# Query norms in a work bank, x transposes one round later, two weight transfers in smaller pieces

## The chip, the core and the metric

The kernel runs on one core of a Trainium2 chip. A core has five engines with instruction queues of their own: PE (TensorE, matrix multiplication), DVE (VectorE), ACT (ScalarE), POOL (GpSimd) and SP (SyncE, which here only issues transfers). They meet at semaphores. PE writes to PSUM[...]; everything else lies in SBUF or in device memory. The metric is the device time of one execution in microseconds.

## The reference, cut to what matters

Attention with normalised queries and keys feeds a layer of experts, in which each token takes one of eight experts besides a dense branch:

```python
q_n, k_n = rmsnorm(q, g_q), rmsnorm(k, g_k)      # (8, 12, 448, 64)
attn = softmax(scale * q_n @ k_n.T)
x = (attn @ v).transpose(0, 2, 1, 3).reshape(B * S, H * D)   # 3584 x 768
y_dense = relu(x @ w1_dense) @ w2_dense           # F = 512
expert_idx = argmax(x @ w_gate, axis=1)           # 8 experts
y_moe[mask] = gate_w[mask] * (relu(x[mask] @ w1[e]) @ w2[e])
return y_dense + y_moe
```

## The kernel before, in words

The kernel has two stages. The first computes attention and, between its own steps, the first half of the dense branch, the router's logits, each token's expert and its place among the expert's tokens. It writes one record per token to device memory. The second stage gathers the records by expert, 128 tokens at a time, and computes the rest. The change touches the first stage, and what both stages call to load weights.

Attention works in groups of four heads, 24 groups in all; three groups make a batch. `period(g)` is one turn of the loop. It has J = 7 rounds (i from 0 to 6), and in each of them PE computes a set of scores for group g + 1 (`scores`, L282) and ACT takes their exp (L285). Besides, the period multiplies the exps of group g with the values in two halves (`attend`, L303, rounds 1 and 2, then 4 and 5), divides each half by its sums (`divide`, L310 and L313, rounds 3 and 6), transposes the queries and keys of group g + 2 (L260, round 3) and copies them out of PSUM (L268, L270, round 4), squares and sums those of g + 3 (L226, L233), turns the sums into norms (`norms`, ACT, L241 to L245) and multiplies queries (DVE) and keys (POOL) with them (`normalise`, L251, round 6). The output x of group g - 2 is transposed (`xtrans`, L323) and copied out (`xturned`, L329).

Work of other kinds comes once per batch. The logits and the choice of expert (L348, L357 to L366) come in round 5 of the third period of a batch, the ranks and places (L383, L392 to L406) in round 5 of the first. The dense branch is done in fills of six matrix multiplications (`fill`, `dense`, L474), each followed by a relu on ACT (`relu`, L485): one at the end of round 6 in every period, and a second one at the end of round 5 in the second period of a batch. Fills begin with the fifth period, logits with the sixth, ranks with the seventh. The norms stop three groups before the end.

The order on every engine is the order in which the code is written: the stage is scheduled by hand, and each engine executes its queue in that order. Waits come from the tiles: an instruction waits for those that use the same tile, or the same buffer of a rotating pool.

[...]The scores have two tiles of two banks. The products with the values have one tile `av` of two banks, each with 260 of its 512 columns in use. The pool `wk` ("work banks") has two banks, handed out in turn to whatever asks next: the x transposes (`xt`), the transposes of queries and of keys (`tr`), the bank `R` of logits or ranks, and each fill (`ff`). Who gets a bank waits until its last reader is done. The norms of the queries, 14 columns, have no bank of their own: they lie behind the products in the first bank of `av` (`rq`, L161). The norms of the keys lie in SBUF.

The weights of the experts come through POOL's queue (`wjobs`), 16 matrices of 1.5 MB read and 768 KB written as bf16. Eleven of them are issued in the periods (L522). The last five lie over memory that the exps use, so they are issued after attention by `late_weight`, which cuts every second matrix, those of the shape 512 x 768, into pieces of one row of 3 KB.

Of the kernel before, what the change touches and what calls it, by code (L numbers as in the profile page):

```python
# [9 lines left out]
F32 = mybir.dt.float32  # L10
# [9 lines left out]
def kernel(  # L20
# [14 lines left out]
    nc = tc.nc  # L35
    P = 128
    B, H, S, D = q.shape
    N = B * S
    Dm = H * D
    E = moe_w_gate.shape[1]  # L40
    F = moe_w1_dense.shape[1]
    J = 7
    NPR = H // 2
    NT = B * NPR
    GP = 2
# [88 lines left out]
        wjobs.append((we[:, e, 1].rearrange("p (fo d) -> p fo d", d=Dm),  # L134
                      moe_w2[e].rearrange("(p fo) d -> p fo d", p=P)))

    def late_weight(i):

        o, w = wjobs[i]
        if i % 2:  # L140
            nc.gpsimd.dma_start(o, w, max_dma_last_dim=4 * Dm)
        else:
            nc.gpsimd.dma_start(o, w)
# [6 lines left out]
    with tc.tile_pool(name="a_ld", bufs=2) as ld, \  # L150
# [4 lines left out]
        tail = [False]  # L155
        xin, sqs, ssqs, rs, xn, qkT, exs, xas, xTs, avs, trs, xps = [{} for _ in range(12)]


        av = avp.tile([P, GP, 512], F32, name="av")
        SP0 = 4 * De  # L160
        rq = av[:, 0, SP0:SP0 + 2 * J].rearrange("p (h j) -> p h j", h=2)  # L161
        def scratch():


# [72 lines left out]
        def norms(g):  # L237
            if g >= NG:
                return
            ln = sb.tile([P, 2, 2, J], F32, tag="ln", name="ln")  # L240
            nc.scalar.activation(ln, ssqs[g], AF.Ln, bias=eps_t, scale=1.0 / D)  # L241
            rs["q"] = rq
            rs["k"] = sb.tile([P, 2, J], F32, tag="r", name="r")
            nc.scalar.activation(rq, ln[:, 0], AF.Exp, scale=-0.5)  # L244
            nc.scalar.activation(rs["k"], ln[:, 1], AF.Exp, scale=-0.5)  # L245
# [60 lines left out]
        def divide(g, hh):  # L306
            b, gb = divmod(g, NPR // GP)
            avv = avs[hh]
            inv = sb.tile([P, GP, 4, 1], F32, tag="inv")
            nc.vector.reciprocal(inv, avv[:, :, :, D:])  # L310
            o = xas[b].rearrange("p m (a c i d) -> p m a i c d", a=NA, c=2, d=D // 2)
            for c in range(2):
                nc.vector.tensor_mul(  # L313
                    o[:, :, gb, 2 * hh:2 * hh + 2, c].rearrange("p m r d -> p r m d"),
                    avv[:, :, :, c * D // 2:(c + 1) * D // 2],
                    inv.to_broadcast([P, GP, 4, D // 2]))
# [177 lines left out]
        def period(g):  # L494
            b, gb = divmod(g, NB)
            for i in range(J):
                if i == 6:
                    divide(g, 1)
                if i > 0:
                    relu()  # L500
                if g + 1 < NG:
                    scores(g + 1, i)
                if i == 0:
                    if g > 1:
                        xtrans(g - 2)
                    squares(g + 3, "k")
                    sums(g + 3, "q")
                if i == 5:
                    if gb == 0 and b > 1:
                        ranks(b - 2)  # L510
                        places(b - 2)
                    if gb == 2 and b > 0:
                        logits(b - 1)
                        choose(b - 1)
                if i in (1, 2, 4, 5):
                    for m in range(2):
                        attend(g, i // 3, (i - 1) % 3 * 2 + m)
                if i == 1:
                    if g > 1:
                        xturned(g - 2)  # L520
                    while nw[0] < len(wjobs) - LATE and (nw[0] - 2) * WPACE <= g + 1:
                        nc.gpsimd.dma_start(*wjobs[nw[0]])  # L522
                        nw[0] += 1
                if i == 3:
                    if g + 2 < NG:
                        transposes(g + 2, "q")
                        transposes(g + 2, "k")
                    divide(g, 0)
                    sums(g + 3, "k")
                    values(g + 2)  # L530
                    squares(g + 4, "q")
                    load(g + 5)
                if i == 4:
                    if g + 2 < NG:
                        turned(g + 2, "q")
                        turned(g + 2, "k")
                if i == 5 and gb == 1:
                    fill(g, KD)
                if i == 6:
                    norms(g + 3)  # L540
                    normalise(g + 3, "q")
                    normalise(g + 3, "k")
                    if gb == 2:
                        store(b, 0, XH, xas[b].bitcast(F32))
                    if gb == 0 and b > 1:
                        gates(b - 2)
                    load_v(g + 4)
                    fill(g, KD)
# [11 lines left out]
        def run(order):  # L560
            with tc.manual_schedule(engines=order):
                for g in range(2):
                    load(g)
                load_v(0)
                load(2)
                load_v(1)
                constants()
                setup()

                squares(0, "q", scalar=True)  # L570
                sums(0, "q")
                squares(0, "k", scalar=True)
                sums(0, "k")
                norms(0)
                normalise(0, "q")
                normalise(0, "k")
                transposes(0, "q")
                transposes(0, "k")
                nc.vector.tensor_mul(gqk, gq2, gk2)
                turned(0, "q")  # L580
                turned(0, "k")
                squares(1, "q", scalar=True)
                sums(1, "q")
                squares(1, "k", scalar=True)
                sums(1, "k")
                values(0)
                squares(2, "q")
                for j in range(J):
                    scores(0, j)
                    if j == 0:  # L590
                        norms(1)
                        normalise(1, "q")
                        normalise(1, "k")
                        load(3)
                        sums(2, "q")
                        squares(2, "k")
                    if j == 2:
                        transposes(1, "q")
                        transposes(1, "k")
                        turned(1, "q")  # L600
                        turned(1, "k")
                        values(1)
                        sums(2, "k")
                        squares(3, "q")
                        load(4)
                    if j == 5:
                        norms(2)
                        normalise(2, "q")
                        normalise(2, "k")
                load_v(2)  # L610
                load_v(3)
                for job in wjobs[:3]:
                    nc.gpsimd.dma_start(*job)
                for g in range(NG - 1):
                    period(g)

                g = NG - 1
                tail[0] = True  # L620
                gts = []
                for i in (-5, -4):
                    late_weight(i)
                for _ in range(2):
                    gts.append(ld.tile([P, 4, RC - GO], F32, tag="xv", name="gt"))
                    nc.gpsimd.memset(gts[-1], 0.0)
                xtrans(g - 2)
                logits(B - 2)
                for hh in range(2):
                    for m in range(4):  # L630
                        attend(g, hh, m)
                    if hh == 0:
                        xturned(g - 2)
                        choose(B - 2)
                        xtrans(g - 1)
                relu()
                divide(g, 0)
                xturned(g - 1)
                ranks(B - 2)
                divide(g, 1)  # L640
                store(B - 1, 0, XH, xas[B - 1].bitcast(F32))
                xtrans(g)
                places(B - 2, (0, 1))
                xturned(g)
                places(B - 2, (2,))
                logits(B - 1)
                fill(g, KD)
                choose(B - 1)
                relu()
                places(B - 2, (3,))  # L650
                ranks(B - 1)
                gates(B - 2, gts[0])
                gates(B - 1, gts[1])
                fill(NG + 1, 8 * KD)
                relu()
                tables()
# [3 lines left out]
    with tc.tile_pool(name="m_sb", bufs=5) as sb, \  # L660
# [76 lines left out]
        def slots(t0, t1):  # L737
# [3 lines left out]
            if t0 == 0:  # L741


                for i in (-3, -2, -1):
                    late_weight(i)
            for t in range(t0 + here, min(t0 + ahead, t1)):
                turn(t)
            turn_here(t0, 0)
# [57 lines left out]
```

## Time and profile before

| | before |
|---|---|
| time, median of 3 runs | 405.2 us (404.52 to 413.1) |
| profiled run, span | 403.5 us |
| PE busy | 344.0 us (85%) |
| DVE, ACT, POOL busy | 226.4, 216.4, 217.3 us |
| granted PE clock | 0.968 |
| attention stage, until its last scores | 224 us |
| PE busy from 50 to 200 us, of 10 us each | 8.24 to 9.86 |

The profile shows one execution. "Busy" is the share of time in which an engine had an instruction in work; for each group of instructions it also tells how long the engine stood idle just before, and which instruction of which engine ended that idle time. In the lines, `xn<-xq,av` means that `xn` was written from `xq` and `av`; L numbers are lines of the kernel before. A row of the timeline gives the start, the duration, the engine, the line and, in brackets, the idle time ahead of it and what ended it. Nearly all of the second stage has PE busy throughout; the attention stage does not.

### The profile page before, as it was taken

What the parts mean: (1) busy time and instruction counts of PE and PEld (TensorE: products, weight loads), DVE (VectorE), ACT (ScalarE), POOL (GpSimd) and SP (SyncE); (2) the same over time, 40 slices, a digit from 0 to 9 for tenths busy, and PEclk for the clock granted to TensorE, in tenths of its full rate; (3) what the DMA queues carried; (4) which work ended last, traced back from release to release, by engine and by line L of the source; (5) the groups of instructions that cost most, each with busy time, mean ns of one, the idle gap of its engine ahead of it and who ended that gap; (6) DMA issues with size and microseconds to landing.
All of it is one profiled execution on the core that took longest, in us unless ns stands there. A gap on an engine that the chain in (4) does not pass through costs nothing. (4 is left out here: it accounts for less than half of the span.)

```text
span 403.5 us, 13022 instructions
## 1 busy us (share of the span) xinstructions
PE 344.0 (85%) x5250; PEld 209.7 (52%) x5250; DVE 226.4 (56%) x554; ACT 216.4 (54%) x349; POOL 217.3 (54%) x193
## 2 busy tenths in 40 slices
PE   0688789989899898899899893799999999999990
PEld 0355565655556555555466542465555555555550
DVE  3856897887978978978786672232212121212220
ACT  4576988778788787787788321122322222222220
POOL 4896797765777676666661102534454545444220
PEclk9996999999999999999999987799999999999997
DMA  7899798959899698899672853999999999999921
GB/s 238 288 249 274 209 257 269 256 144 334 193 280 259 187 255 259 224 278 237 187 159 72 144 137 84 216 259 239 253 252 225 231 266 225 253 249 212 224 104 51
DMA packets 79372, 88.08 MB, mean 218 GB/s; under 512 B 44109, under 2 KB 71245, under 8 KB 79312
## 3 DMA queue, kind: packets, MB, share of 16 engines
q1 hardware_dynamic: 67424, 51.30, 48.9%
q0 software_dynamic: 11568, 35.93, 36.5%
q8 instruction: 44, 0.72, 0.7%
q14 instruction: 16, 0.13, 0.1%
q10 hardware_dynamic: 320, 0.00, 0.0%
HBM read 72.12 MB, written 21.99 MB: 233 GB/s over the span
## 5 line engine op out<-in xcount | busy, mean ns | idle before, releaser
L285 ACT ACTIVATE we<-sc 128x896 bf16<-128x896 f32 x168 | 147.6, 919 | 27.7 <-PE sc L282 27.1
L303 PE MATMUL av<-va,we 64*128 64x65 bf16 x2576 | 59.1, 194 | 15.9 <-DVE xn L251 13.5
L251 POOL TENSOR_TENSOR xn<-xk,r 128x896 bf16<-128x896 f32 x24 | 40.5, 1689 | 58.6 <-issue 45.5
L282 PE MATMUL sc<-y 64*64 64x448 bf16 x672 | 67.2, 392 | 4.8 <-ACT we L285 3.9
L726 DVE COPY ys<-yp 128x384 f32<-128x384 f32 x32 | 17.8, 558 | 94.8 <-issue 89.8
L728 POOL DMA_INDIRECT out_dram<-ys,dest x32 | 32.4, 1013 | 71.0 <-ACT ys L727 53.6
L303 PEld LDWEIGHTS <-we 64*128 64x128 bf16 x2688 | 51.0, 96 | 33.3 <-issue 32.2
L233 DVE TENSOR_REDUCE ssq<-sq 128x14 f32<-128x896 f32 x48 | 51.7, 1078 | 3.9 <-ACT sq L224 2.8
L668 POOL DMA_INDIRECT xg<-records,row x32 | 31.4, 982 | 33.6 <-issue 33.6
L727 ACT COPY ys<-yp 128x384 f32<-128x384 f32 x32 | 15.3, 479 | 63.4 <-PE yp L720 53.6
L693 PE MATMUL he<-we,xT 128*128 (+1 forms) x192 | 47.8, 386 | 1.2 <-issue 0.6
L698 ACT ACTIVATE hs<-he,xg 128x512 bf16<-128x512 f32 x32 | 22.0, 687 | 48.9 <-PE he L693 46.1
L474 PE MATMUL ff<-wd,xT 128*128 128x512 bf16 x192 | 47.6, 388 | 0.0
L714 PE MATMUL yp<-wd,xT 128*128 128x384 bf16 x256 | 46.8, 326 | 0.0
L720 PE MATMUL yp<-we,heT 128*128 (+1 forms) x256 | 46.8, 326 | 0.0
L226 POOL TENSOR_TENSOR sq<-xq 128x896 f32<-128x896 f32 x22 | 37.0, 1684 | 4.3 <-DMA xq<-in_q_dram 2.4
L251 DVE TENSOR_TENSOR xn<-xq,av 128x896 bf16<-128x896 f32 x24 | 26.1, 1088 | 21.8 <-ACT av L244 21.8
L226 POOL TENSOR_TENSOR sq<-xk 128x896 f32<-128x896 f32 x22 | 37.0, 1682 | 0.0
L260 PE MATMUL tr<-ident,xn 128*128 128x128 bf16 x336 | 25.9, 235 | 11.9 <-DVE xn L251 11.9
L313 DVE TENSOR_TENSOR xa<-av,inv 128x256 bf16<-128x256 f32 x92 | 34.7, 419 | 1.6
L282 PEld LDWEIGHTS <-y 64*64 64x64 bf16 x672 | 20.0, 105 | 29.2 <-issue 18.4
L714 PEld LDWEIGHTS <-xT 128*128 128x128 bf16 x256 | 24.9, 98 | 19.0
(120 smaller groups left out, 359.1 us busy)
## 6 DMA issues: line engine op xcount, KB each, us to landing
we<-in_moe_w_dram POOLq DMA_DIRECT2D x16, 768.0 KB
xq<-in_q_dram SPq DMA_DIRECT2D x24, 448.0 KB, 7.5
xk<-in_k_dram SPq DMA_DIRECT2D x24, 448.0 KB, 7.0
xv<-in_v_dram SPq DMA_DIRECT2D x24, 448.0 KB, 6.4
records<-xa SPq DMA_DIRECT2D x16, 288.0 KB, 5.0
records<-we SPq DMA_DIRECT2D x44, 64.0 KB, 3.6
wd<-in_moe_w_dense_dram POOLq DMA_DIRECT2D x2, 768.0 KB
records<-xa SPq DMA_DIRECT2D x8, 96.0 KB, 4.8
```

The lines of the kernel that those rows point to most:

```text
L226: nc.gpsimd.tensor_mul(sqs[name, g], x, x)
L233: nc.vector.tensor_reduce(ssqs[g][:, "qk".index(name)], sqs[name, g].rearrange("p h (j d) -> p h j d", d=D), AX.X, ALU.add)
L251: (nc.vector if name == "q" else nc.gpsimd).tensor_mul(y.rearrange("p j h d -> p h j d"), xin[name, g].rearrange("p h (j d) -> p h j d", d=D),
L282: nc.tensor.matmul(ps[r * D:(r + 1) * D, hh, :S], kT[rows, r, j], qT[rows, r].rearrange("p j s -> p (j s)"), start=True, stop=True)
L285: nc.scalar.activation(x, ps[:, :, :S], AF.Exp, scale=scale)
L303: nc.tensor.matmul(avv[:, r, m], exs[g, j][rows, hh, QC[m]:QC[m] + P], va[rows, hh, j, :De], start=(j == 0), stop=(j == J - 1))
L313: nc.vector.tensor_mul(o[:, :, gb, 2 * hh:2 * hh + 2, c].rearrange("p m r d -> p r m d"), avv[:, :, :, c * D // 2:(c + 1) * D // 2], inv.t ...
L474: nc.tensor.matmul(ff[0], xTs[b][:, kk, QC[m]:QC[m] + P], wd1[:, kk], start=(kk == 0), stop=(kk == KD - 1))
L693: nc.tensor.matmul(he, xTs[t][:, kk], we[:, bass.ds(eregs[t], 1), 0, kk * F:(kk + 1) * F] .rearrange("p o f -> p (o f)"), start=(kk == 0), ...
L714: nc.tensor.matmul(yp[dd], xTs[t][:, KD + i], wd2[:, i, dd * HD:(dd + 1) * HD], start=(i == 0), stop=False)
L720: nc.tensor.matmul(yp[dd], heTs[t][:, i], we[:, bass.ds(eregs[t], 1), 1, i * Dm + dd * HD:i * Dm + (dd + 1) * HD] .rearrange("p o f -> p ( ...
L728: i = nc.gpsimd.indirect_dma_start(out=out, out_offset=bass.IndirectOffsetOnAxis(ap=dest[:, t:t + 1], axis=0), in_=ys.rearrange("p a d -> ...
```

## The change

There are three edits.

1. The norms of the queries move out of the values' banks. Each call of `norms` takes the next work bank for them. With this, the first products of a period no longer wait for the multiplication of the queries, which reads those norms. The call itself moves ahead of the second division, to the beginning of round 6, so that ACT need not stand behind the sixth exp.
2. The x transposes move from round 0 to the end of round 2, with their copy directly behind them instead of in round 1. Round 0 then has only its scores on PE, and the products follow at once.
3. `late_weight` takes the tiles instead of an index and decides by the shape. In the periods it is used for every weight from the tenth index on, so that two more matrices (the second ones of experts 3 and 4) are read in pieces of 3 KB. The aim is that long pieces do not hold up other transfers.

```diff
-    def late_weight(i):
-        o, w = wjobs[i]
-        if i % 2:
+    def late_weight(o, w):
+        if o.shape[-1] == Dm:
             nc.gpsimd.dma_start(o, w, max_dma_last_dim=4 * Dm)
         else:
             nc.gpsimd.dma_start(o, w)
...
-        SP0 = 4 * De
-        rq = av[:, 0, SP0:SP0 + 2 * J].rearrange("p (h j) -> p h j", h=2)
...
-            rs["q"] = rq
+            rq = wkp.tile([P, 512], F32, tag="wk", name="rq")[:, :2 * J]
+            rq = rs["q"] = rq.rearrange("p (h j) -> p h j", h=2)
...
                 if i == 6:
+                    norms(g + 3)
                     divide(g, 1)
...
                 if i == 0:
-                    if g > 1:
-                        xtrans(g - 2)
                     squares(g + 3, "k")
                     sums(g + 3, "q")
...
+                if i == 2 and g > 1:
+                    xtrans(g - 2)
+                    xturned(g - 2)
                 if i == 1:
-                    if g > 1:
-                        xturned(g - 2)
                     while nw[0] < len(wjobs) - LATE and (nw[0] - 2) * WPACE <= g + 1:
-                        nc.gpsimd.dma_start(*wjobs[nw[0]])
+                        (late_weight if nw[0] > 9 else nc.gpsimd.dma_start)(*wjobs[nw[0]])
                         nw[0] += 1
...
                 if i == 6:
-                    norms(g + 3)
                     normalise(g + 3, "q")
                     normalise(g + 3, "k")
```

More of the change, by code (lines that the diff above doesn't have):

```diff
@@ L622, in run @@
                 for i in (-5, -4):
-                    late_weight(i)
+                    late_weight(*wjobs[i])
                 for _ in range(2):
@@ L744, in slots @@
                 for i in (-3, -2, -1):
-                    late_weight(i)
+                    late_weight(*wjobs[i])
             for t in range(t0 + here, min(t0 + ahead, t1)):
```

## The prediction

> **What bounds the kernel now.** I read the page by slices first: the change touches only the attention stage, which runs from the first scores to about 226 us. There no engine is full, so I asked for three consecutive periods (one per group of four heads; a batch has three). The columns are PE, PEld, DVE, ACT and POOL busy, clock, DMA share, GB/s.
>
> ```profile
> 108.73:118.72 9.99, 8.70 (x176) 5.09 (x175) 7.77 (x19) 7.54 (x13) 5.96 (x4) 1.00 1.00 263
> 118.72:127.22 8.50, 8.03 (x193) 5.33 (x192) 7.54 (x19) 7.05 (x12) 6.53 (x5) 1.00 0.93 248
> 127.22:135.68 8.46, 7.64 (x177) 4.92 (x177) 7.76 (x21) 7.01 (x11) 5.91 (x4) 1.00 0.93 273
> ```
>
> Three periods last 26.95 us; PE is busy 24.36, DVE 23.07. PE leads, and DVE is so near that its delays come back as waits of PE. The list of waits names the largest (us, times, longest):
>
> ```profile
> ACT we L285 <- PE sc L282: 27.1, 46, 2.4
> DVE xn L251 <- ACT av L244: 21.8, 24, 2.3
> PE av L303 <- DVE xn L251: 13.5, 14, 1.3
> ```
>
> ACT waits for PE, not PE for ACT, so PE and its waits set the period. The third line is what the change aims at. The timeline shows its making (start, us):
>
> ```profile
> 109.06 0.76 DVE L313 TENSOR_TENSOR xa<-av,inv 128x256 bf16<-128x256 f32 x2
> ...
> 109.91 0.19 ACT L244 ACTIVATE av<-ln 128x14 f32<-128x14 f32 x1 [1.34 <-DVE xa L313]
> ...
> 110.13 1.09 DVE L251 TENSOR_TENSOR xn<-xq,av 128x896 bf16<-128x896 f32 x1 [0.31 <-ACT av L244]
> ...
> 111.27 0.62 PE L303 MATMUL av<-va,we 64*128 64x65 bf16 x28 [1.29 <-DVE xn L251]
> ```
>
> The queries' norms lie in the bank of the values' products: ACT waits for DVE's division, DVE for ACT, and PE for both. This wait is 1.29 after a period with ranks, about 0.2 after one with two fills, 0.49 after one with logits: 1.98 us per three periods. Last, the end of a period with ranks:
>
> ```profile
> 133.15 0.18 PE L383 MATMUL R<-oh,tri 128*128 128x32 bf16 x1 [0.34 <-DVE y L268]
> ...
> 133.43 0.61 PE L303 MATMUL av<-va,we 64*128 64x65 bf16 x28
> ...
> 133.97 0.38 PE L282 MATMUL sc<-y 64*64 64x448 bf16 x4
> ...
> 134.28 1.47 PE L474 MATMUL ff<-wd,xT 128*128 128x512 bf16 x6
> ...
> 135.11 0.76 DVE L406 TENSOR_SCALAR sel<-iop,R 128x128 f16<-128x128 bf16 x4
> ```
>
> DVE reads bank R until 135.87, and PE starts the fill (ff) at 134.28, in the other work bank.
>
> [...]ACT L244 waits for xa L313 on disjoint columns. [...]so a fill that waits for its bank holds back the next period's scores. The 1.29 us above has this form.[...]
>
> **The change, part by part.** Steps on PE, start to start in these rows: a set of scores 0.31, an attend pair 0.55, x transposes 0.55, the 14 q and k transposes 0.88, a fill 1.40, logits 0.67, ranks 0.28. A PE result is seen about 0.12 after the next step could start (0.07 drain, 0.05 to the waiter).
>
> *Norms in a work bank.* It removes the 1.98 us. Placed ahead of the sixth round's exp, the three ACT instructions (0.31, 0.19, 0.20) fall into ACT's idle before that exp (1.01 and 0.61 us in the rows at 125.95 and 134.40): no cost. But the norms now take a turn in the two work banks. Each period now hands out six: xt, tr q, tr k, R or first fill, norms, fill. In the changed program the last fill thus gets the bank of R, or of the first fill; before, it got the other. New waits, on PE, with the next scores queued behind:
> - Ranks: DVE's last read ends 135.87 - 133.50 = 2.37 after the ranks end, that is 0.28 + 0.07 + 2.37 + 0.05 = 2.77 after they start. PE gets there after 0.28 + 0.55 + 0.31 = 1.14. Wait 1.63.
> - Logits: the last read is 126.48 - 125.04 = 1.44 after their end; 0.67 + 0.07 + 1.44 + 0.05 = 2.23 against 1.53. Wait 0.70.
> - Two fills: the relu (0.60) stands between; 1.40 + 0.07 + 0.05 + 0.60 + 0.05 = 2.17 against 1.71. Wait 0.46.
>
> *x transposes in the third round.* The work is the same, but DVE's copy out (0.61) now stands ahead of the first division and waits for PE. Call X the end of the x transposes on PE. DVE copies from X+0.12, goes on 0.52 later, reciprocal 0.24, the products end at X+1.63; the k sums start at X+1.55, take 1.00, the copy of q 0.67: X+3.22. PE: scores, q transposes, k transposes (from X+0.75, when the copy has emptied their bank), scores: X+1.50; the second half's attend waits to X+1.68 (0.18, before none); then attend and scores: X+2.54. Logits and ranks need the bank of q: X+3.27, a wait of 0.73 (before 0.33). The first fill of a two-fill period needs it too: 0.18. X itself: two scores, one attend, and then scores that need the first exp, 0.38 + 0.05 + 0.92 + 0.05 = 1.40 into the period (wait 0.23); 1.40 + 0.31 + 0.55 + 0.55 = 2.81.
>
> *Sum by period:*
> - Logits: 2.81 + 3.27 + 0.67 + 0.55 + 0.31 + 0.70 + 1.40 = 9.71 (before 8.5).
> - Ranks: 2.81 + 3.27 + 0.28 + 0.55 + 0.31 + 1.63 + 1.40 = 10.25 (before 8.46).
> - Two fills: 2.81 + 3.27 + 1.40 + 0.31 + 0.46 + 1.40 = 9.65 (before 9.99, and its large wait is gone).
>
> 29.61 against 26.95: 2.66 more per batch. By the starts of the Ln row (L241): the batch from 55.68 to 81.32 took 25.64, so +3.97; three took about 26.95 (81.32 to 108.26, 108.26 to 135.22, 162.89 to 189.85): +7.98; 135.22 to 162.89, disturbed, 27.67: +1.94; the two periods to 209.00 took 10.79 and 8.36: -1.14 and +1.35. The last two periods have no norms and DVE is freer: -0.4. The first four have no fills: the 1.16 us wait goes, but the norms now wait for the copy of k, X+3.76 on DVE, and delay the sixth exp; worked through ACT that gives 7.24 against 7.28: nothing. Total +13.7 us. What follows attention starts later by that and is otherwise unchanged.
>
> *Weights in 3 KB pieces.* Two more transfers (the second matrices of experts 3 and 4). Issuing costs POOL 0.78 us in this form (L143, two) and 0.82 in the plain form (L141): nothing. PE stood 0.47 us at 197.66 "<-issue" while such a transfer was in flight; if smaller pieces end that, the gain is about 0.5 us, and I have taken it above (9.65 for the period of 10.79). Bounds: 0 to 1 us.
>
> **Rivals.**
> - Forecast (0.68): all of these waits show; 405.2 + 13.7 = 418.9.
> - A wash (0.16): DVE catches up, so only the three waits for fills' banks are new: 2.79 - 1.98 = 0.8 per batch, some 5.5 batches, 4.5 us: 410, up to 413 with part of the DVE delay. For it: DVE idles 2.02 us before xn in one period of three. Against: that idle time lies in another round.
> - Faster (0.09): the fills' waits hide behind something that PE would wait for anyway; then 1.98 x 5.5 = 11 us go: 394. For it: the 13.5 us are real. Against: PE runs fills back to back with scores, and the bank's last reader is fixed by the program.
> - Much slower (0.07): delays also reach the k transposes and the exps, another 0.3 to 0.5 per period in 20 periods: 425 to 429.
>
> **How the numbers follow.** 2% is 8.1 us: 397.1 and 413.3. Forecast and much slower: 0.75 slower; wash 0.16; faster 0.09. The range 409 to 425 takes the forecast with 6 us above it and most of the wash; it leaves out the faster case, the lower end of the wash, and the much slower one, together below 0.2.
>
> **What would show it.** In the changed profile: the wait of av L303 for xn gone; new waits of ff on DVE's sel (about 1.6 us, five times), on oh (0.7, six) and on ACT's relu (0.5, six); R waiting 0.7 for y instead of 0.33; batches of 29 to 30 us between Ln rows; a longer attention stage with PE's busy share lower. I am wrong if the fills follow the scores without a gap, or if R starts earlier than 3 us after the x transposes.

## The result and the profile after

| | before | after |
|---|---|---|
| time, median | 406.25 us (404.52 to 413.1) | 445.73 us (440.83 to 453.18) |
| ratio, 95% interval | | 1.0947 [1.0813, 1.1081] |
| profiled run, span | 403.5 us | 444.9 us |
| granted PE clock | 0.968 | 0.918 |

The medians are of all executions of a kernel; the ratios, here and below, leave out those more than 1.5% above the kernel's fastest.

The kernel became slower, as forecast, but by 39.5 us where 13.7 were forecast. The extra time lies in the attention stage. The `Ln` of `norms` (L241 before, L238 after) marks the periods; the seventh of its 24 instructions stands at the end of the last period without a fill. The stage ends where PE first multiplies with `sel` (L448, L446):

| stretch, us | before | forecast, against before | after |
|---|---|---|---|
| to the seventh Ln | 55.68 | 0 | 54.09 (-1.6) |
| next batch | 25.64 | +3.97 | 26.63 (+1.0) |
| four batches | 108.53 | +9.92 | 139.20 (+30.7) |
| two periods | 19.15 | +0.21 | 23.38 (+4.2) |
| to the end of the stage | 34.06 | -0.4 | 38.88 (+4.8) |
| second stage | 160.4 | 0 | 162.7 (+2.3) |

In the kernel after, Ln stands earlier in its period, ahead of the fill; the rows at either end are shifted by that, and the four batches compare cleanly. One batch of the kernel after, to be held against the first lines of the prediction, in three stretches from Ln to Ln. The first begins between the ranks and their fill (us, then PE, PEld, DVE, ACT and POOL busy, PE clock, DMA share, GB/s):

```profile
80.72:96.34 15.62, 10.29 (x202) 5.98 (x200) 12.04 (x26) 7.34 (x13) 6.53 (x5) 0.78 0.68 159
96.34:105.95 9.61, 8.21 (x154) 4.91 (x154) 6.46 (x13) 7.59 (x13) 5.89 (x4) 1.00 0.70 207
105.95:115.68 9.73, 8.06 (x197) 5.39 (x194) 7.71 (x20) 7.11 (x12) 6.71 (x5) 1.00 0.67 149
```

34.96 us where 29.61 were forecast, and the stretch behind the ranks carries all of it; it also has a lower clock. The list of waits of the kernel after (us in total, times, longest):

```profile
ACT we L283 <- PE sc L280: 75.4, 64, 7.4
...
PE ff L472 <- DVE sel L404: 20.9, 5, 5.2
...
PE R L346 <- DVE y L266: 3.9, 6, 0.7
PE ff L472 <- DVE oh L363: 3.8, 6, 0.6
...
PE R L381 <- DVE y L266: 3.3, 5, 0.7
...
PE ff L472 <- ACT we L483: 2.2, 6, 0.4
```

The products' wait for xn has gone, and all the forecast waits are there. Four are within 0.1 us of their forecast size. One, of the fill for `sel`, is 3.6 to 5.2 us where 1.63 was forecast. Its timeline on PE:

```profile
80.51 0.18 PE L381 MATMUL R<-oh,tri 128*128 128x32 bf16 x1 [0.66 <-DVE y L266]
...
81.33 0.38 PE L280 MATMUL sc<-y 64*64 64x448 bf16 x4
86.67 0.61 PE L472 MATMUL ff<-wd,xT 128*128 128x512 bf16 x1 [4.96 <-DVE sel L404]
87.50 1.91 PE L472 MATMUL ff<-wd,xT 128*128 128x512 bf16 x4 [0.22 <-issue]
...
90.23 0.95 PE L301 MATMUL av<-va,we 64*128 64x65 bf16 x28
```

The fill starts 6.16 us after the ranks, and then needs about 2.7 us, where it took 1.47 before; the products take 0.95 instead of 0.61. So there are two losses here, a longer wait and slower matmuls after it. What DVE did in the wait:

```profile
82.27 0.17 DVE L400 SCALAR_TENSOR_TENSOR R<-tj,R 128x4 f32<-128x4 f32 x1
82.47 4.14 DVE L404 TENSOR_SCALAR sel<-iop,R 128x128 f16<-128x128 bf16 x4
86.53 0.19 DVE L308 RECIPROCAL inv<-av 128x8 f32<-128x8 f32 x1
```

The four instructions that took 0.76 before take 4.14. DVE was not late: it began them 1.96 us after the ranks had started, as before (135.11 - 133.15). They themselves became long. POOL in the same stretch of the kernel after:

```profile
81.53 1.69 POOL L249 TENSOR_TENSOR xn<-xk,r 128x896 bf16<-128x896 f32 x1 [3.78 <-PE av L301]
83.17 1.68 POOL L223 TENSOR_TENSOR sq<-xk 128x896 f32<-128x896 f32 x1
84.80 0.61 POOL L520 DMA_DIRECT2D we<-in_moe_w_dram  x1
85.41 0.98 POOL L211 CAST va<-xv 128x896 bf16<-128x896 f32 x1
```

Taken one by one in narrow windows, the first `sel` ends at 83.27, just after POOL's xn (83.22), the second at 84.91, just after sq (84.85), the third at 86.45, just after the cast (86.39). The third began at 84.83, while POOL issued a transfer, and was held through that and the cast. In another batch POOL stands idle after sq (it ends at 119.82), and `sel` is shorter:

```profile
117.43 2.77 DVE L404 TENSOR_SCALAR sel<-iop,R 128x128 f16<-128x128 bf16 x4
118.14 1.68 POOL L223 TENSOR_TENSOR sq<-xk 128x896 f32<-128x896 f32 x1
```

In the kernel before, in the period with ranks that the prediction shows, POOL's xn began after `sel` had ended (135.87):

```profile
137.31 1.69 POOL L251 TENSOR_TENSOR xn<-xk,r 128x896 bf16<-128x896 f32 x1 [3.34 <-DMA xk<-in_k_dram]
```

So in this batch the long `sel` instructions end 0.05 to 0.06 us after the POOL instructions that they ran beside. The small steps on bank R aren't held up: the one ahead of `sel` (L400, 0.17) has POOL's xn beside it and takes as long as in the kernel before (L402, 0.17). Why POOL holds up the one and not the other, no trace here shows.

The clock, by windows of the kernel after around this wait (same columns as above):

```profile
81.40:86.60 5.20, 0.31 (x4) 0.04 (x4) 5.03 (x10) 1.03 (x2) 4.85 (x4) 0.86 0.59 175
86.60:89.30 2.70, 2.41 (x5) 0.73 (x6) 2.63 (x8) 0.00 (x0) 0.00 (x0) 0.50 0.96 177
89.30:92.30 3.00, 3.00 (x69) 1.73 (x68) 0.49 (x1) 2.32 (x4) 1.68 (x1) 0.55 0.50 92
```

In the wait PE's clock is 0.86; behind it, it is 0.50 and then 0.55, for more than 5 us in all. In other runs below, some matmuls are slow behind waits of 0.64 to 1.97 us as well. Over the whole stage, from the seventh Ln to the first product with `sel`, before and then after:

```profile
55.68:243.06 187.38, 168.44 (x3641) 104.86 (x3638) 153.13 (x402) 140.14 (x227) 109.97 (x83) 0.99 0.82 216
```

```profile
54.09:282.18 228.09, 182.96 (x3628) 110.92 (x3649) 164.98 (x403) 143.49 (x228) 110.48 (x83) 0.90 0.70 178
```

Of 40.7 us more, 14.5 are PE busy longer with the same matmuls, and 26.2 are PE standing idle.

### The profile page after: what moved, and what is told of

Read it like the earlier page. It is cut to its first block, busy times and chain, and to the rows that moved or that the text cites. A ratio compares the mean times of both kernels' runs of the same rounds, so it can differ in the third digit from the quotient of the medians.

```text
span 444.9 us, 12987 instructions
## 1 busy us (share of the span) xinstructions
PE 356.3 (80%) x5214; PEld 214.9 (48%) x5250; DVE 237.2 (53%) x554; ACT 218.5 (49%) x349; POOL 217.8 (49%) x193
## 5 line engine op out<-in xcount | busy, mean ns | idle before, releaser
L472 PE MATMUL ff<-wd,xT 128*128 128x512 bf16 x172 | 54.3, 442 | 29.9 <-DVE sel L404 20.9
L301 PEld LDWEIGHTS <-we 64*128 64x128 bf16 x2688 | 52.8, 98 | 26.6 <-issue 25.9
L301 PE MATMUL av<-va,we 64*128 64x65 bf16 x2576 | 60.8, 197 | 3.7 <-issue 1.5
L690 PE MATMUL he<-we,xT 128*128 (+1 forms) x176 | 44.8, 386 | 5.0 <-DMA xT<-xg 3.1
L472 PEld LDWEIGHTS <-xT 128*128 128x128 bf16 x192 | 19.2, 107 | 53.4 <-DVE sel L404 22.2
L327 DVE COPY xT<-xt 128x896 bf16<-128x896 bf16 x24 | 15.0, 624 | 54.7 <-PE xt L321 54.7
```

The lines of the kernel that those rows point to most:

```text
L301: nc.tensor.matmul(avv[:, r, m], exs[g, j][rows, hh, QC[m]:QC[m] + P], va[rows, hh, j, :De], start=(j == 0), stop=(j == J - 1))
L472: nc.tensor.matmul(ff[0], xTs[b][:, kk, QC[m]:QC[m] + P], wd1[:, kk], start=(kk == 0), stop=(kk == KD - 1))
L690: nc.tensor.matmul(he, xTs[t][:, kk], we[:, bass.ds(eregs[t], 1), 0, kk * F:(kk + 1) * F] .rearrange("p o f -> p (o f)"), start=(kk == 0), ...
```

## The experiments

The explanation tested: the early norms release POOL's multiplication of the keys before `sel`; POOL then blocks `sel`, the fill waits for its bank, and the clock falls behind the wait. Rivals: the turn of the banks alone is dearer than worked out; the x transposes are; or the clock falls for a reason of its own. Each ratio is to the kernel before on the same chip, with its 95% interval.

### Is it the place of the norms?

**e1_norms_old_place**, on the kernel after:

```diff
                 if i == 6:
-                    norms(g + 3)
                     divide(g, 1)
...
                 if i == 6:
+                    norms(g + 3)
                     normalise(g + 3, "q")
```

> The changed kernel with one thing undone: the call of norms stands again behind the sixth exp, where it stood in the kernel before; the norms of the queries stay in a work bank. Theory: DVE's four sel instructions[...] stretch from 0.76 to 2.8 to 4.3 us because POOL's multiplication of the keys now runs at the same time, and it does so because the norms come early. With the norms behind the exp, POOL starts about 1.5 us later, most of the sel instructions are done by then: sel 0.8 to 1.5 us, the wait of the fill 1.6 to 2.4 us instead of 3.6 to 5, no drop of the PE clock behind it, batches of 30 to 31 us instead of 34 to 36, time 418 to 426. Rival (the norms' turn in the work banks alone is the cost, and sel is slow for another reason such as transfers): sel stays at 2.8 us or more, time 438 to 448.

424.12 us (420.2 to 429.19), ratio 1.044 [1.0341, 1.054], clock 0.957. Its DVE, POOL and PE rows:

```profile
80.41 0.76 DVE L404 TENSOR_SCALAR sel<-iop,R 128x128 f16<-128x128 bf16 x4
```

```profile
81.31 1.69 POOL L249 TENSOR_TENSOR xn<-xk,r 128x896 bf16<-128x896 f32 x1 [3.42 <-ACT eg L367]
```

```profile
81.22 1.47 PE L472 MATMUL ff<-wd,xT 128*128 128x512 bf16 x6 [1.57 <-DVE sel L404]
```

POOL starts after `sel` again, `sel` takes 0.76, the fill waits 1.57, near the forecast 1.63, and takes 1.47. The four batches take 29.61, 31.09, 31.00 and 29.62; forecast was 29.61. The two long ones have one fill of 2.74 instead of 1.47, that of the logits. So about 21 us of the loss (the ratio falls from 1.095 to 1.044) hang on where one call stands.

**e7_keys_norms_early**, on the kernel before: only the keys' norms move ahead, the queries' stay.

```diff
                 if i == 6:
+                    norms(g + 3)      # Ln and the keys' exp alone
                     divide(g, 1)
...
                 if i == 6:
-                    norms(g + 3)
+                    norms_q(g + 3)    # the queries' exp
```

> The kernel before, with one thing added: the norms of the keys alone (Ln and one Exp) come ahead of the second division and the sixth exp, as in the changed kernel; those of the queries, the x transposes, the banks and the weights are as before. POOL's multiplication of the keys then starts before DVE's sel. Theory: sel stretches from 0.76 to 2 us or more in the batches with ranks (five times), the division and with it the products of the next period come later by as much; time 410 to 420. Rival (POOL does not disturb sel): sel stays at 0.76 us, time within 1% of before.

425.35 us (424.98 to 434.56), ratio 1.0429 [1.0384, 1.0474], clock 0.930. Its DVE and PE rows:

```profile
81.28 4.44 DVE L415 TENSOR_SCALAR sel<-iop,R 128x128 f16<-128x128 bf16 x4
```

```profile
85.77 0.62 PE L332 MATMUL xt<-ident,xa 128*128 128x128 bf16 x8 [3.54 <-DVE sel L415]
```

Neither the new tile nor the x transposes' new place nor the pieces are in this kernel, and yet `sel` takes 3.06 to 4.63 us; the next user of bank R, here the x transposes, waits. The mechanism needs nothing else of the change. The time is above the 410 to 420 expected; the clock, which the expectation left out, fell too.

**e2_keys_norms_late**, on the kernel after: the opposite, the keys' exp and POOL's xn behind the first exp of the next period.

```diff
                 if i == 0:
+                    norms_k(g + 2)
+                    normalise(g + 2, "k")
                     squares(g + 3, "k")
...
                     normalise(g + 3, "q")
-                    normalise(g + 3, "k")
```

> The changed kernel, with the norms of the queries as early as in it, but the last step of the keys' norms (one ACT instruction of 0.2 us) and POOL's multiplication of the keys moved behind the first exp of the next period. POOL then has nothing to do while DVE works on sel. Theory (POOL beside sel is the excess over the forecast): all sel groups take 0.76 us, the fills wait 1.6 us for sel, batches take 29.6 to 30.5 us as forecast, time 417 to 423. Rival (the bank in which sel's operand lies, or transfers, make sel slow): sel stays at 2.8 us or more and the time within 2% of the changed kernel's, 438 to 450.

442.66 us (437.08 to 447.84), ratio 1.0895 [1.0796, 1.0995]. `sel` is back at 0.76 and its fill at 1.57, but the keys now come too late. From its list of waits:

```profile
PE R L353 <- DVE y L273: 7.5, 6, 1.2
```

1.2 us at bank R where the kernel after has 0.7, and nine fills of 2.25 to 2.74 us. One wait was exchanged for others; as a test of the total the run failed, as the 417 to 423 expected were missed by 20 us. What it shows is that `sel` is short when POOL is out of its way.

### The bank or POOL?

**e4_places_in_sbuf**, on the kernel after: the places that `sel` compares lie in SBUF, so that R's last reader is ahead of `sel`.

```diff
+            if 2 in steps:
+                trs["lof", b] = sb.tile([P, 4], F32, tag="lof", name="lof")
+            lof = trs.get(("lof", b))
```

> The changed kernel, with the four numbers per partition that sel reads as its operand (lof) in SBUF instead of the work bank R. The bank is then free when the places are computed, 0.8 us after DVE has started on them less than 2 us after the ranks, and the fill no longer waits for sel; but the division behind sel on DVE still does, and so the next products. Theory: sel stays long (2 to 4.3 us, as POOL is still beside it), the fill's wait falls to about 0.9 us, and what it saves comes back in part as a wait of the products for the division; time 428 to 440. Rival (the bank's wait is the whole loss): most of the loss goes, time 410 to 420.

431.63 us (430.84 to 433.99), ratio 1.0598 [1.054, 1.0656]. A DVE row, then one of PE:

```profile
84.02 3.15 DVE L407 TENSOR_SCALAR sel<-iop,lof 128x128 f16<-128x128 bf16 x4
```

```profile
88.12 0.62 PE L301 MATMUL av<-va,we 64*128 64x65 bf16 x28 [2.11 <-DVE xa L311]
```

The fill no longer waits for `sel` (its wait, for lof, is 1.8 at most, where 0.9 was expected), but `sel` stays long, and what DVE has queued behind it, the second division, now holds up PE. Freeing the bank moves the wait and doesn't remove its cause.

**e9_sel_two_inputs**, on the kernel after: the same comparison in another form, with one operand in SBUF and the other in PSUM.

```diff
-                    nc.vector.tensor_scalar(sel[:, b, m], iop, lof[:, m:m + 1], None,
-                                            op0=ALU.is_equal)
+                    nc.vector.tensor_tensor(sel[:, b, m], iop,
+                                            lof[:, m:m + 1].to_broadcast([P, P]), ALU.is_equal)
```

> The changed kernel, with DVE's sel written as a tensor_tensor comparison (iop against lof, broadcast from PSUM) instead of a tensor_scalar: same work on 128 x 128, one operand in SBUF, one in PSUM. POOL's multiplication of the keys stays as early as it is in the changed kernel. Theory[...]: sel takes 0.2 to 0.3 us each beside POOL, the fill's wait falls to 1.5 to 1.9 us, no drop of the PE clock, time 417 to 424. Rival (POOL slows whatever DVE does in SBUF): sel stays above 0.5 us on average and the time above 432.

426.03 us (423.61 to 428.1), ratio 1.0485 [1.0419, 1.0551], clock 0.943. Its DVE row, POOL's at that time, then two of PE:

```profile
83.31 0.88 DVE L404 TENSOR_TENSOR sel<-iop,R 128x128 f16<-128x128 bf16 x4
```

```profile
82.37 1.69 POOL L249 TENSOR_TENSOR xn<-xk,r 128x896 bf16<-128x896 f32 x1 [3.40 <-PE av L301]
84.02 1.68 POOL L223 TENSOR_TENSOR sq<-xk 128x896 f32<-128x896 f32 x1
```

```profile
84.25 2.74 PE L472 MATMUL ff<-wd,xT 128*128 128x512 bf16 x6 [1.70 <-DVE sel L404]
...
116.19 1.47 PE L472 MATMUL ff<-wd,xT 128*128 128x512 bf16 x6 [1.70 <-DVE sel L404]
```

POOL's xn and sq run over the whole of `sel`, from 83.31 to 84.19, and don't delay it: this form, with the other operand in PSUM, takes 0.88 for four in all six groups, also in the last (237.67), where the norms have stopped. The norms stand early as in the kernel after, so it is the form of `sel` beside POOL, not the early norms as such. No fall of the clock was expected; but behind the same wait of 1.70 the fill takes 2.74 in three batches and 1.47 in two, and four batches take 31.94, 29.74, 31.87 and 29.73. That is also why the time lies above the 417 to 424 expected.

### The clock

**e11_delay_alone**, on the kernel of e1: `sel` written five times over, to delay the fill without POOL.

```diff
-                for m in range(4):
-                    nc.vector.tensor_scalar(sel[:, b, m], iop, lof[:, m:m + 1], None,
-                                            op0=ALU.is_equal)
+                for m in range(4 if tail[0] else 20):
+                    nc.vector.tensor_scalar(sel[:, b, m % 4], iop, lof[:, m % 4:m % 4 + 1],
+                                            None, op0=ALU.is_equal)
```

> The changed kernel with the norms at the old place, and the four sel instructions written five times over, with the same values: DVE is held up by about 2.7 us once per batch (five to six times), with POOL out of the way. It puts in the delay that POOL causes in the changed kernel (2.0 to 3.6 us per batch) by other means. Theory (the delay is what matters, and PE's long idle makes the granted clock drop to half for some 4 to 6 us behind it): the fill waits 4.2 to 4.5 us, the clock drops behind each of these waits, and the time is near that of the changed kernel, 438 to 449, that is more than the delay alone, 424 + 5.5 x 2.7 = 439, would give. Rival (the clock has nothing to do with the wait): no drop behind the waits, time 436 to 440.

466.91 us (465.05 to 468.19), ratio 1.15 [1.1435, 1.1565], clock 0.901. Its DVE row, then PE's:

```profile
81.09 7.54 DVE L404 TENSOR_SCALAR sel<-iop,R 128x128 f16<-128x128 bf16 x20
```

```profile
88.69 2.74 PE L472 MATMUL ff<-wd,xT 128*128 128x512 bf16 x6 [8.35 <-DVE sel L404]
```

The delay grew to more than twice what was meant. In e1, with the norms in the same place, POOL's xn starts 0.90 us after the first `sel` (81.31 - 80.41), so this is probably not a delay without POOL, and its total, far above the 438 to 449 expected, separates nothing. The fills behind the five long waits, 7.9 to 8.6 us, all take 2.74.

**e14_pe_kept_busy**, on the kernel after: 14 matmuls that nothing reads fill PE's wait in the five periods with ranks and a norm.

```diff
+                    if gb == 0 and b > 1 and g + 3 < NG:
+                        busy = scp.tile([P, 2, 512], F32, tag="sc", name="busy")
+                        for n in range(14):
+                            nc.tensor.matmul(busy[:, 0], ident, wd1[:, 0], start=True, stop=True)
                     fill(g, KD)
```

> The changed kernel, in which PE computes 14 matrix multiplications of 128 x 512 (0.24 us each at full clock, 3.3 us in all) into a scores' tile that nobody reads, once in each of the five periods with ranks, directly ahead of the fill that waits for sel. Its wait is 3.6 to 5.2 us there, so they fit in. DVE, ACT and POOL do what they do in the changed kernel. Theory (the granted clock drops to half because PE stands idle, and that costs 2 to 3 us per batch on top of the wait): the rows behind the wait run at full clock, a fill in 1.47 us instead of 2.7, batches 2 us shorter; time 430 to 438 against 441 to 447 for the changed kernel. Rival (the clock's drop has another cause, such as power or the transfers, or costs nothing since PE waits anyway): time 441 to 450.

438.79 us (436.22 to 440.08), ratio 1.082 [1.0751, 1.0888], clock 0.951. PE has extra work, and the median is 6.9 us below that of the kernel after; but the two ran on different chips and the intervals of their ratios overlap, so the stretches of the profiles tell more. PE's rows:

```profile
83.23 3.19 PE L548 MATMUL busy<-wd,ident 128*128 128x512 bf16 x14
88.26 1.47 PE L472 MATMUL ff<-wd,xT 128*128 128x512 bf16 x6 [1.83 <-DVE sel L404]
...
107.61 2.74 PE L472 MATMUL ff<-wd,xT 128*128 128x512 bf16 x6 [0.64 <-DVE oh L363]
```

`sel` is as long as in the kernel after, but all five fills behind it take 1.47. From the start of the fill to the x transposes PE takes 3.66 us (88.26 to 91.92), where the kernel after took 5.64 (86.67 to 92.31). So behind these waits it is PE's idleness that makes the matmuls slow. Part is given back: in three of the four batches the fill of the logits, two periods later, is slow, against two in the kernel after. The four batches take 133.2 us, against 139.2.

### The edits one by one

**e5_bank_alone**, on the kernel before: edit 1's tile, nothing moved.

```diff
-            rs["q"] = rq
+            rq = wkp.tile([P, 512], F32, tag="wk", name="rq")[:, :2 * J]
+            rq = rs["q"] = rq.rearrange("p (h j) -> p h j", h=2)
```

> The kernel before with the move of the queries' norms into a work bank alone: the call stays where it was, the x transposes stay in round 0, the weights as before. The forecast's steps: fills wait 1.63, 0.70 and 0.46 us for their bank as in the changed kernel, R waits 0.33 as before, the products no longer wait for the queries' multiplication, but the x transposes do, since their bank was that of the norms. Sum: about +1.0 to +1.5 us per batch; time 409 to 415. Rival (the later x transposes are harmless and the bank's turn is the whole of what is left without POOL's part): as slow as the kernel with the norms at the old place, 420 to 424.

417.07 us (414.64 to 422.64), ratio 1.0259 [1.0197, 1.0322], above the 409 to 415 expected. The fills wait 1.50 for `sel`, 0.57 for oh and 0.37 for the relu, about 0.1 less than worked out. In the profiled run, the slowest of the four, some fills behind 1.50 take 2.4 to 2.7 us, which the expectation hadn't counted; whether the others have as many isn't known.

**e6_xt_late_alone**, on the kernel before: edit 2.

```diff
                 if i == 0:
-                    if g > 1:
-                        xtrans(g - 2)
...
+                if i == 2 and g > 1:
+                    xtrans(g - 2)
+                    xturned(g - 2)
                 if i == 1:
-                    if g > 1:
-                        xturned(g - 2)
```

> The kernel before with the later x transposes alone; the norms stay in the values' bank. The products still wait for the queries' multiplication, now longer by the 0.55 us that the x transposes filled, three times per batch, and DVE's copy stands ahead of the first division: R waits 0.73 instead of 0.33. By the forecast's steps +2.5 to 3 us per batch, in the batches with and without fills: time 418 to 426. Rival (the place of the x transposes does not matter, as the work on PE is the same): 404 to 409.

430.26 us (429.12 to 433.27), ratio 1.0629 [1.0567, 1.069], more than expected. PE's rows of a batch:

```profile
119.66 0.62 PE L303 MATMUL av<-va,we 64*128 64x65 bf16 x28 [1.97 <-DVE xn L251]
...
120.53 0.95 PE L303 MATMUL av<-va,we 64*128 64x65 bf16 x28
```

Without the x transposes in round 0, PE comes to the products sooner and waits longer for xn: 26.5 us in all, against 13.5 before. The costs of e5 and e6 don't add up to e1's, and this is a reason: edit 1 removes the wait that edit 2 enlarges. Here too the second products behind the 1.97 us run slowly (0.95).

**e10_pieces_alone**, on the kernel before: edit 3.

```diff
-                        nc.gpsimd.dma_start(*wjobs[nw[0]])
+                        (wpieces if nw[0] > 9 and wjobs[nw[0]][0].shape[-1] == Dm else nc.gpsimd.dma_start)(*wjobs[nw[0]])
```

> The kernel before with the third edit alone: two more weights read in pieces of 3 KB. The forecast put it at 0 to 1 us of gain. Theory: within 1 us of before, 404.5 to 407. Rival (smaller pieces slow the weights and so other transfers, or they end PE's waits for instructions): more than 2 us either way.

404.81 us (402.18 to 411.29) against 407.54, ratio 0.9939 [0.9912, 0.9966]: about 2.5 us gained (1.4 to 3.6). That is more than the 0 to 1 us of the prediction, and beyond the 1 us that the theory allowed. It doesn't come by the way named there: the wait "<-issue" that smaller pieces were to end, 0.47 us before, is 1.37 us here at the same place. In the profiles 1.0 us is gained in the attention stage and 0.9 behind it; what brings it stays open.

### A better order

**e8_fill_first**, on the kernel after: the fill takes its bank ahead of the norms, so that the turn of the banks is as before; norms behind the sixth exp; x transposes in round 2, ahead of the products.

```diff
                 if i == 6:
-                    norms(g + 3)
                     divide(g, 1)
...
+                if i == 2 and g > 1:
+                    xtrans(g - 2)
+                    xturned(g - 2)
                 if i in (1, 2, 4, 5):
...
                 if i == 6:
+                    fill(g, KD)
+                    norms(g + 3)
                     normalise(g + 3, "q")
...
                     load_v(g + 4)
-                    fill(g, KD)
```

> A version that keeps the aim and avoids both losses: norms of the queries in a work bank, but the last fill of a period takes its bank before the norms do, so that it gets the one that was emptied long ago; the norms stand behind it and behind the sixth exp, so POOL starts after sel; the x transposes stand in round 2 ahead of the second pair of products, so DVE copies them before the first division is due. Theory: the fills wait for nothing, the products wait for the division alone, sel stays at 0.76 us; about 0.9 us less per batch than before, time 398 to 404. Rival (some other wait takes its place, such as the x transposes for the relu, whose bank they get): 405 to 412.

398.41 us (396.98 to 402.57), ratio 0.9842 [0.979, 0.9894], clock 0.975: 1.6% below the kernel before. PE in a period with ranks:

```profile
75.75 0.61 PE L301 MATMUL av<-va,we 64*128 64x65 bf16 x28
76.29 0.38 PE L280 MATMUL sc<-y 64*64 64x448 bf16 x4
76.61 1.47 PE L472 MATMUL ff<-wd,xT 128*128 128x512 bf16 x6
78.01 0.57 PE L280 MATMUL sc<-y 64*64 64x448 bf16 x8
79.15 0.62 PE L301 MATMUL av<-va,we 64*128 64x65 bf16 x28 [0.57 <-DVE xa L311]
```

The fill follows the scores with no wait, the first products wait 0.57 for the division instead of 1.29 for xn, and three periods take 26.14 us. So the aim of edit 1 was right; the bank's turn and the two moves around it undid it. Edit 3 is part of this version; the next run leaves it out.

**e12_fill_first_no_pieces**, e8 without edit 3:

```diff
-                        (late_weight if nw[0] > 9 else nc.gpsimd.dma_start)(*wjobs[nw[0]])
+                        nc.gpsimd.dma_start(*wjobs[nw[0]])
```

> The version with the fill ahead of the norms, without the pieces of 3 KB in the periods. Theory (the pieces do next to nothing): within 1.5 us of that version, 397 to 400. Rival: above 401.

401.9 us (398.57 to 405.77), ratio 0.9885 [0.9828, 0.9941]. The order alone is 1.2% below the kernel before. The time is above the 397 to 400 expected, but the interval overlaps that of e8: inconclusive on the pieces beside this order.

**e13_fill_first_router_last**, e8 with logits and ranks behind the products of round 5:

```diff
+                if i in (1, 2, 4, 5):
+                    for m in range(2):
+                        attend(g, i // 3, (i - 1) % 3 * 2 + m)
                 if i == 5:
...
-                if i in (1, 2, 4, 5):
-                    for m in range(2):
-                        attend(g, i // 3, (i - 1) % 3 * 2 + m)
```

> The version with the fill ahead of the norms, with logits or ranks (and the DVE work on them) behind the pair of products of round 5 instead of ahead of it. PE then has the products to do while DVE empties the bank that R gets, so R's wait of 0.33 us goes; DVE starts its router work about 0.2 us later. Theory: 0.3 to 0.6 us less per batch, 395 to 398. Rival (the later division holds up the next products by as much): 398 to 400.

400.74 us (398.08 to 402.9), ratio 0.9872 [0.9823, 0.9921]: no gain over e8, where 395 to 398 us were expected. R no longer waits, but from its list of waits

```profile
PE av L301 <- DVE xa L311: 8.7, 13, 1.0
```

where e8 has 3.8 us, 7 times: the wait has moved.

## Why the prediction was right in direction and wrong in size

**What held.** Edit 1 removes the wait for xn and gives the fills new ones; edit 2 delays R. Measured against forecast: R 0.65 to 0.66 (0.73), fills 0.64 for oh (0.70), 0.37 for the relu (0.46), and, where PE's clock holds, the period of the logits from scores to scores (99.65 to 109.38) 9.73 (9.71). The fill for `sel`, once POOL is out of the way, waits 1.57 (1.63), and e1's undisturbed batches take 29.61 and 29.62 (29.61). e1's profiled run is 15.0 us longer than before, for a forecast of 13.7; by the ratio e1 is about 18 longer. The nearness of 15.0 is partly luck: up to the seventh Ln e1 gained 2.8 us where nothing was forecast, and in the two periods behind the four batches it lost 3.4 where 0.2 was. That edits 1 and 2 each cost time alone is shown by e5 and e6. The forecast's statement that nothing changes after attention holds to 2.3 us. Of edit 3 it had two things wrong that hardly weigh: the gain was larger and not by the way named (e10), and in the kernel before L141 issues the form in pieces (0.82) and L143 the plain one (0.78), not the other way round.

**The step that failed.** "Placed ahead of the sixth round's exp, the three ACT instructions ... fall into ACT's idle before that exp ...: no cost." The prediction looked at the engine that was moved and not at what its result releases. The keys' norm is the third of those instructions. On ACT itself the step was right, as the exp still waits for PE:

```profile
81.20 0.20 ACT L243 ACTIVATE r<-ln 128x14 f32<-128x14 f32 x1
81.76 0.92 ACT L283 ACTIVATE we<-sc 128x896 bf16<-128x896 f32 x1 [0.36 <-PE sc L280]
```

The norm ends at 81.40, and POOL, which had stood idle for 3.78 us, starts at 81.53, one microsecond ahead of `sel`. (Its row names products of PE that ended at 81.39 as what released it; in e1 it is the later norm that POOL follows, by the same 0.13 us: 81.18, then 81.31.) `sel` was costed at the row of before, 0.76, which was measured with POOL idle. e1 (move undone), e7 (move alone) and e9 (another form of `sel`) show this from three sides.

**The term that was missing.** The forecast priced every wait at its own length. Over the four batches the kernel after took 5.19 us per batch more than forecast (34.80 against 29.61). The waits for `sel` there average 4.32, which is 2.69 over the forecast; the other 2.50 are about what the slow matmuls add: about 2.0 behind the wait for `sel` (5.64 against 3.66 in the batch shown), and about 1.1 at the fill of the logits in two of the four. e14 wins back 1.5 of these 2.50 by keeping PE busy in the wait. Behind waits of the size forecast matmuls can be slow as well (e5, e6, e9, and two of e1's four batches).

**The rivals.** "Wash" and "faster" fell on the fills' waits, which showed in full. "Much slower" was on the right side for a wrong reason: it added delays of the k transposes and exps, and at 425 to 429 was still 17 us short. The range missed since no case held a slower clock (0.918 for 0.968), or DVE held up by POOL (`sel` 4.14 us for 0.76).

**What stays open.** Which wait slows the matmuls behind it isn't settled. In e9, 1.70 us did in three cases of five, while before's 1.29 showed none in the rows read. In e1 the fill of the logits, behind the same wait, was fast in one batch and slow in the next:

```profile
100.58 1.47 PE L472 MATMUL ff<-wd,xT 128*128 128x512 bf16 x6 [0.64 <-DVE oh L363]
...
130.19 2.74 PE L472 MATMUL ff<-wd,xT 128*128 128x512 bf16 x6 [0.64 <-DVE oh L363]
```

PE's rows in the 19 us ahead of the two are alike, in work and in waits, so something that these rows don't show decides between them. How the last few microseconds divide between the stages wasn't separated either.

## What to carry to other kernels

When an instruction moves earlier, follow its result to whoever it releases, and ask which instructions of other engines that work will now lie beside: here `sel` took 0.76 us with POOL idle and 4.14 beside three of its instructions, so the duration in the row of before didn't hold for the kernel after. A wait on TensorE may cost more than its length, as what follows it may run slowly: here a fill took 2.74 us instead of 1.47 behind every wait of 3.6 us and more for `sel`, and in some cases behind 1.5 to 1.7. And a new tile in a rotating pool changes who waits for whom at every later turn: count the turns first, and if possible let the urgent user (here the fill) take its turn before the newcomer, as in e8.

## What the runs showed of the hardware

- One `sel` instruction took 0.25 us in the kernel before and up to 1.8 us beside POOL in the kernel after; the long ones in the batch shown end 0.05 to 0.06 us after a POOL instruction of 1.0 to 1.7 us. The chain of four took 2.77 us beside two of these, 4.14 and 4.34 beside three and a transfer's issue.
- The same comparison as a tensor_tensor with one operand in PSUM took 0.88 us for four, beside POOL's xn and sq (83.31) as in the last group, where the norms have stopped (237.67; e9).
- PE's matmuls took nearly twice their time (a fill 2.74 us instead of 1.47) behind idle times of 1.5 to 1.7 us in some cases (e5, e9), and behind all of 3.6 us and more for `sel`, where the trace of the kernel after shows a clock of 0.50. With 14 unread matmuls in the wait the fill took 1.47, and four batches 133.2 us instead of 139.2 (e14). Behind the same wait of 0.64 us, a fill was fast once (1.47) and slow once (2.74; e1).
- Reading two more 1.5 MB weights in pieces of 3 KB shortened the kernel by 0.6% [0.3%, 0.9%] (e10).
